# Groups of three score units instead of two, with x copied by VectorE in the first row

## Chip, cores, metric

One core of a Trainium2 chip. The time is device microseconds of one execution, the median of several. All runs used here were in the fast state, except that before_again is a single execution, whose state is not known. The calls to the chip ran on different chips, each with its own runs of before, so kernels of different calls are compared by their ratios. A ratio is the mean time of one kernel's fast runs over that of the other's fast runs of the same rounds, so it is not quite the ratio of the medians that are quoted.

## The reference

Attention with a threshold, then an MLP mixer, all in f32:

```python
# q, k, v: (8 batches, 8 heads, 576, 64)
scores = (q @ k.T) / 8
scores = where(scores >= max(scores) - tau, scores, -1e9)
attn   = softmax(scores)
x      = (attn @ v), heads side by side          # (8, 576, 512)
h      = relu(x.T @ w_tok1) @ w_tok2             # token mixer
u      = x + h.T
out    = u + relu(u @ w_ch1) @ w_ch2             # channel mixer
```

## The kernel before

Heads go in pairs. Two pairs make a quad of 2 x 576 = 1152 query rows, cut into nine **units** of 128 rows; the fifth unit is shared, 64 rows of each pair. Eight batches with two quads each are 16 quads, 144 units. I call the 18 units of one batch a **row of units**. A unit's life: TensorE makes scores, VectorE takes maxima, ScalarE makes e, GpSimd scales it. Then e must be turned, so that its keys lie on partitions. One unit later in the first row, two in the later ones, the finished group meets v in a **visit** of values, which gives x.

The first row (b=0) has no mixer work yet; there e is turned by TensorE through PSUM and copied. From the second row on it is turned in 32x32 blocks by VectorE, and 16 transfers put the blocks in place:

```python
def group_of(u):                      # units are visited two at a time, the shared one alone
    b, p0, t = units[u]
    if t == SHARED:
        return (b, p0, "s"), 0, 1
    i, c = divmod(t - (t > SHARED), NI)
    return (b, p0 + i, c // 2), c % 2, 2

def turn(u, third):                   # first row, cut
    ps = ps_tr.tile(...)              # two PSUM buffers, shared with the visits
    for c in range(3):
        nc.tensor.transpose(out=ps[:, c, :], in_=e[:, k0 : k0 + P], identity=ident)
    on = nc.scalar.copy if third == 1 and u % 2 else nc.vector.tensor_copy
    on(out=eT[...], in_=ps)

def turn_blocks(u):                   # later rows, cut
    nc.vector.transpose(out=T[...], in_=e[...])
    if place == n - 1:
        eTs[key] = work.tile([P, NK * 2 * P], F32, tag="eT")      # two buffers
        for a in range(4):
            for i in range(4):
                nc.sync.dma_start(out=eTs[key][...], in_=T[...])

def values(b, p, c):                  # a visit, cut: N = 256 columns, or 64 for the shared unit
    ps = ps_tr.tile(...)
    for h in range(2):                # the two heads: two 64-column halves of the array, side by side
        nc.tensor.matmul(to[r], lhsT=vl[:, r], rhs=eT[:, NI], start=True, ...)
    for c in range(NI):
        for h in range(2):
            nc.tensor.matmul(to[r], lhsT=lv[:, j, :], rhs=eT[:, j], ...)
    nc.scalar.copy(out=x, in_=ps)
```

One iteration of the main loop, cut to the order of work:

```python
scores(u)
values_due(u)                 # first row
norm(u - 1)
turn(w, 0..2)                 # first row, w = u - 2
fill(0.4)                     # mixer products of the batch before, from the second row on
turn_blocks(w)                # later rows
weight_to(2.25 * (u - 1.5))   # first row: a few steps of unpacking the mixer's weights, mostly VectorE
weigh(u)                      # e, with fill(0.2) between its parts
...
load_qk(...); prep(...)       # q and k of a later pair: loads, VectorE turns them
values_due(u)                 # later rows: just ahead of the next scores
```

## Time and profile before

| | before |
|---|---|
| median of the first 6 runs | 1381.45 us (1379.32 to 1383.14) |
| records of TensorE for visits | 1920 |
| transfers of e | 1120 |

The prediction shows the page's slices and where TensorE is idle. One more view is needed here: busy time in three stretches that follow the program, namely the first row of units, the second row, and the rest (from the first scores of units 0, 18 and 36). Columns: length, then busy time of TensorE, its weight loads, VectorE, ScalarE, GpSimd, then granted clock, DMA share and GB/s.

```profile
9.73:100.58 90.85, 77.67 (x504) 48.25 (x504) 71.26 (x146) 66.75 (x145) 46.20 (x84) 0.96 0.46 106
100.58:260.18 159.60, 139.28 (x731) 86.78 (x730) 113.97 (x177) 90.51 (x194) 78.70 (x105) 0.95 0.52 137
260.18:1381.30 1121.12, 1113.38 (x5636) 699.09 (x5632) 402.87 (x680) 431.71 (x989) 227.86 (x482) 1.00 0.35 85
```

In the first row VectorE is busy 71.3 of 90.9 us. What ends its idle time there, from the waits of VectorE in that window (total us, times, longest):

```profile
DVE eT L362 <- PE tr L360: 10.9, 18, 1.4
DVE mx L309 <- PE sc L304: 7.2, 6, 2.4
```

It waits for TensorE, in pieces of at most 2.4 us.

### The profile page before, as it was taken

The numbers are of one execution on the slowest core, as the hardware profiler recorded it, in microseconds if no ns is written. First come the engines' busy times: TensorE is split into PE (matmuls) and PEld (weight loads), VectorE is DVE, ScalarE is ACT, GpSimd is POOL, SyncE is SP. The second block draws the span as 40 slices with busy tenths as digits, with TensorE's granted clock in tenths as the row PEclk, the third lists the DMA queues.
The fourth block names the chain that finished last, engine by engine and source line by source line (L and its number), as shares of the span: only waits on it lengthen the run. The fifth ranks groups of instructions, "written<-read, shape, count | busy, mean of one in ns | idle before, by whom it ended". The sixth has DMA issues, their size and how long they took to land.

```text
span 1381.3 us, 19492 instructions
## 1 busy us (share of the span) xinstructions
PE 1330.3 (96%) x6866; PEld 834.1 (60%) x6866; DVE 590.3 (43%) x1009; ACT 589.5 (43%) x1328; POOL 354.8 (26%) x683
## 2 busy tenths in 40 slices
PE   6887789999999999999999999999999999999998
PEld 3544555646565666665766567565657566575675
DVE  5889875354444443434244444433343453201000
ACT  5776654445445444443434444353434454120110
POOL 3556653232323222222222222221221232100000
PEclk9988999999999999999999999999999999999999
DMA  5444654453444444433433444443333433300000
GB/s 118 109 105 120 180 150 119 109 129 89 110 121 105 98 110 101 105 81 88 109 87 93 104 95 107 99 102 81 94 90 92 110 74 88 83 8 16 8 8 23
DMA packets 257376, 128.34 MB, mean 93 GB/s; under 512 B 208064, under 2 KB 221376, under 8 KB 257280
## 3 DMA queue, kind: packets, MB, share of 16 engines
q1 hardware_dynamic: 129264, 111.16, 30.6%
q10 hardware_dynamic: 128016, 15.94, 7.3%
q8 instruction: 55, 0.90, 0.3%
q14 instruction: 41, 0.34, 0.1%
HBM read 43.25 MB, written 9.44 MB: 38 GB/s over the span
## 4 chain that ended last, share of the span: by engine, by line
PE 88%; DVE 6%; DMA 2%; SPq 1%; issue 1%; ACT 1%; POOL 1%; ACTq 0%; DVEq 0%; POOLq 0%
PE c L487 27%; PE c L471 27%; PE sc L304 11%; PE pv L416 8%; PE t L442 4%; PE t L449 4%; PE pv L411 3%; DVE mx L309 2%; PE c L483 1%; PE tx L433 1%; SPq L381 1%; PE pv_s L416 1%; DVE eT L362 1%; PE tr L360 1%; DMA eT<-T 1%
## 5 line engine op out<-in xcount | busy, mean ns | idle before, releaser
L309 DVE TENSOR_REDUCE mx<-sc 128x1 f32<-128x576 f32 x288 | 204.6, 751 | 488.6 <-PE sc L304 488.6
L471 PE MATMUL c<-xT,wc 128*128 128x256 f32 (+1 forms) x1920 | 401.0, 363 | 6.2 <-ACT g L472 5.0
L487 PE MATMUL c<-wc,g 128*128 128x512 f32 x864 | 390.7, 597 | 0.0
L471 PEld LDWEIGHTS c<-xT,wc 128*128 128x128 f32 x1920 | 335.0, 191 | 76.5 <-issue 29.0
L310 POOL TENSOR_SCALAR bias<-mx,toff 128x1 f32<-128x1 f32 x288 | 79.2, 275 | 803.1 <-DVE mx L309 746.5
L487 PEld LDWEIGHTS c<-wc,g 128*128 128x128 f32 x864 | 157.4, 190 | 175.6 <-issue 173.6
L319 ACT ACTIVATE e<-sc,bias 128x576 f32<-128x576 f32 x288 | 198.8, 739 | 141.4 <-POOL bias L310 141.2
L472 ACT ACTIVATE g<-c 128x256 f32<-128x256 f32 (+1 forms) x240 | 86.9, 362 | 328.8 <-PE c L471 315.4
L337 POOL TENSOR_SCALAR e<-e,rr 128x576 f32<-128x576 f32 x288 | 217.2, 767 | 16.8 <-DVE rr L334 4.7
L326 ACT ACTIVATE e<-e,ntau 128x576 f32<-128x576 f32 x288 | 220.8, 771 | 0.0
L304 PE MATMUL sc<-kT,qT 64*128 64x288 f32 (+1 forms) x1280 | 196.5, 441 | 15.0 <-DVE kT L286 9.7
L371 DVE STREAM_TRANSPOSE T<-e 128x1152 f32<-128x1152 f32 x126 | 172.6, 1370 | 13.3 <-DMA eT<-T 8.5
L304 PEld LDWEIGHTS sc<-kT,qT 64*128 64x128 f32 (+1 forms) x1280 | 107.3, 181 | 91.8 <-issue 44.8
L416 PE MATMUL pv<-eT,lv 128*64 128x256 f32 x1024 | 124.9, 386 | 0.0
L492 DVE COPY o<-c 128x512 f32<-128x512 f32 x36 | 24.9, 692 | 174.5 <-PE c L487 174.5
L416 PEld LDWEIGHTS pv<-eT,lv 128*64 128x64 f32 x1024 | 75.9, 140 | 39.0 <-issue 3.6
L421 ACT COPY xT<-pv 128x256 f32<-128x256 f32 x64 | 23.8, 372 | 174.8 <-PE pv L416 167.0
L449 PE MATMUL t<-w,a 128*128 128x288 f32 x256 | 75.2, 421 | 6.3 <-DVE xT L453 4.3
L442 PE MATMUL t<-x_sb,w 128*128 128x512 f32 x160 | 72.1, 597 | 0.0
L449 PEld LDWEIGHTS t<-w,a 128*128 128x128 f32 x256 | 46.0, 192 | 31.3 <-issue 11.5
L453 DVE TENSOR_TENSOR xT<-xT,t 128x288 f32<-128x288 f32 x64 | 28.2, 446 | 78.1 <-PE t L449 77.4
L326 ACT ACTIVATION_READ_ACCUMULATOR e<-e,ntau 128x1 f32 x288 | 56.6, 196 | 0.0
(48 smaller groups left out, 604.3 us busy)
## 6 DMA issues: line engine op xcount, KB each, us to landing
eT<-T SPq DMA_DIRECT2D x896, 72.0 KB, 2.0
scratch<-in_moe_w_ch_dram SPq DMA_DIRECT2D x24, 512.0 KB, 3.7
lv<-in_v_dram SPq DMA_DIRECT2D x32, 288.0 KB, 3.4
out_dram<-o SPq DMA_DIRECT2D x36, 256.0 KB, 2.1
lk<-in_k_dram ACTq DMA_DIRECT2D x112, 72.0 KB, 2.7
eT<-T SPq DMA_DIRECT2D x224, 36.0 KB, 1.9
lq<-in_q_dram ACTq DMA_DIRECT2D x104, 72.0 KB, 2.2
lq<-in_q_dram SPq DMA_DIRECT2D x24, 72.0 KB, 3.4
```

What stands on the lines that cost most here:

```text
L304: nc.tensor.matmul(sc[h][rows, f, 0:HS], lhsT=qT[r, cols], rhs=kT[r, HS * f : HS * f + HS], start=True, stop=True)
L309: nc.vector.tensor_reduce(out=mx[:, c], in_=sc[h][:, :, 0:HS], axis=AX.XY, op=ALU.max)
L319: nc.scalar.activation(out=eh, in_=sc[h][:, :, 0:HS], func=AF.Prelu, bias=bias[:, h : h + 1], scale=SCALE, alpha=STEEP)
L326: nc.scalar.activation(out=eh, in_=eh, func=AF.Exp, bias=ntau, accum_out=rs[:, h : h + 1])
L337: nc.gpsimd.tensor_scalar(out=eh, in0=eh, scalar1=rr[:, h : h + 1], scalar2=1.0, op0=ALU.mult, op1=ALU.mult)
L371: nc.vector.transpose(out=T.rearrange("p (a c n x) -> p c a n x", a=4, c=NK, n=n)[:, :, :, place, :], in_=e.rearrange("p (c a x) -> p c a ...
L416: nc.tensor.matmul(to[r], lhsT=lv[:, j, :], rhs=eT[:, j], start=False, stop=(c == NI - 1), skip_group_check=True)
L442: nc.tensor.matmul(ps, lhsT=w1[:, t, P * m : P * m + P], rhs=x_sb[:, t, :], start=(t == 0), stop=(t == NT - 1))
L449: nc.tensor.matmul(ps, lhsT=s["a"][:, m, P * c : P * c + P], rhs=w2[:, m, HS * f : HS * f + HS], start=(m == 0), stop=(m == NTK - 1))
L471: nc.tensor.matmul(ps, lhsT=wc1[:, j, c, :], rhs=uT[:, c, GR * i : GR * i + n], start=(c == 0), stop=(c == NCC - 1))
L472: nc.scalar.activation(out=s["g"][:, j, 0:n], in_=ps, func=AF.Relu)
L487: nc.tensor.matmul(flat, lhsT=s["g"][:, j, P * t : P * t + P], rhs=wc2[:, j, :], start=False, stop=(j == NJ - 1), skip_group_check=True)
```

## The change

Three units make a group, the shared one among them, so a quad has three visits instead of five: 384, 2 x 192 and 384 columns; in the shared unit the second pair now gives its first 64 rows, no longer its last. There are 48 transfers of e a quad instead of 80. Because the buffers grow, e turned has one buffer instead of two in the later rows, and q and k have one instead of two, so they are loaded later. In the first row VectorE copies x, and the weight steps stand ahead of the turning.

```diff
-    def group_of(u): ...
+    GU = 3
+    key, place = (b, p0, t // GU), t % GU
...
-    for i in range(4): ... eTs[key][32 * a : 32 * a + 32, w * i : w * i + w] <- T[32 * i : 32 * i + 32, w * a : w * a + w]
+    eT = work.tile([P, GU, 4, NK * 32], F32, tag="eT", bufs=1)
+    for i in range(4): ... eT[32 * a : 32 * a + 32, :, i, :] <- T[32 * i : 32 * i + 32, a, :, :]
...
+    SHARES = [[(0, 0, GU * P, 0)], [(0, 0, P + LAST, 2 * P + P), (1, P + LAST, P + LAST, 0)], [(1, 0, GU * P, P + LAST)]]
+    def values(b, p0, g): ... for i, first, N, tok in SHARES[g]: (ten products of N columns)
...
-        nc.scalar.copy(out=x, in_=ps)
+            if in_blocks(b):
+                nc.scalar.copy(out=x, in_=ps)
+            else:
+                copies.append(lambda x=x, ps=ps: nc.vector.tensor_copy(out=x, in_=ps))
...
         norm(u - 1)
+        weight_to(2.25 * (u - 1.5))          # first row
+        while copies: copies.popleft()()
         turn(w, 0..2)
-        weight_to(2.25 * (u - 1.5))
...
-        loaded[n] = [ld.tile([P, S // 32, 32], F32, tag=tag) ...]              # two buffers
+        loaded[n] = [ld.tile([P, S // 32, 32], F32, tag=tag, bufs=1) ...]
-        load q and k five or more units ahead, the second pair's at the very start
+        when = {3: (2, 0, 2), 4: (2, 2, 4), 5: (2, 4, 6), 6: (2, 6, 8), 8: (3, 0, 3), 0: (1, 3, 6), 1: (1, 6, 8)}
```

More of the change, by code (lines that the diff above doesn't have):

```diff
@@ L95, with load_qk @@
     vlast = [const.tile([P, P], F32, name=f"vl{i}") for i in range(VL)]
-    def load_qk(n, eng, part=None):
+    def load_qk(n, eng, parts=range(8)):
         b, p = pairs[n]
         if n not in loaded:
-            loaded[n] = [ld.tile([P, S // 32, 32], F32, tag=tag, name=f"{tag}_{n}") for tag in ("lq", "lk")]
-        for i in range(4) if part is None else (part,):
+            loaded[n] = [ld.tile([P, S // 32, 32], F32, tag=tag, bufs=1, name=f"{tag}_{n}") for tag in ("lq", "lk")]
+        for part in parts:
+            i, which = divmod(part, 2)
             h, c = divmod(i, 2)
-            for src, t, on in zip((q, k), loaded[n], eng):
-                on.dma_start(
-                    out=t[32 * i : 32 * i + 32], in_=src[b, 2 * p + h, :, 32 * c : 32 * c + 32].rearrange("(n t) d -> t n d", t=32)
-                )
+            eng[which].dma_start(
+                out=loaded[n][which][32 * i : 32 * i + 32],
+                in_=(q, k)[which][b, 2 * p + h, :, 32 * c : 32 * c + 32].rearrange("(n t) d -> t n d", t=32),
+            )
     def load_v(n):
@@ L245 @@
     load_piece(0)
-    load_qk(1, (nc.sync, nc.scalar))
-    load_piece(1)
     load_v(0)
-    for i in range(2, NRAW):
+    for i in range(1, NRAW):
         load_piece(i)
@@ L295, in scores @@
         if t == SHARED:
-            parts = [(b * NP + p0 + i, slice(MAIN, S), slice(64 * i, 64 * i + 64)) for i in range(2)]
+            parts = [(b * NP + p0, slice(MAIN, S), slice(0, 64)), (b * NP + p0 + 1, slice(0, LAST), slice(64, P))]
         else:
-            i, c = divmod(t - (t > SHARED), NI)
-            parts = [(b * NP + p0 + i, slice(P * c, P * c + P), slice(0, P))]
+            o = P * t if t < SHARED else LAST + P * (t - SHARED - 1)
+            parts = [(b * NP + p0 + (t > SHARED), slice(o, o + P), slice(0, P))]
         order = [(f, part, h) for f in range(2) for part in parts for h in range(2)]
@@ L338, in norm, with turn @@
         st[u] = e
-    def group_of(u):
+    GU = 3
+    def turn(u, third):
         b, p0, t = units[u]
-        if t == SHARED:
-            return (b, p0, "s"), 0, 1
-        i, c = divmod(t - (t > SHARED), NI)
-        return (b, p0 + i, c // 2), c % 2, 2
-    def turn(u, third):
-        key, place, n = group_of(u)
+        key, place = (b, p0, t // GU), t % GU
         e = st[u]
         if third == 0 and place == 0:
-            eTs[key] = work.tile([P, NK * 2 * P], F32, tag="eT", name=f"eT_{u}")
+            eTs[key] = work.tile([P, NK, GU * P], F32, tag="T", name=f"eT_{u}")
         if third == 2:
             st.pop(u)
-        eT = eTs[key][:, 0 : NK * n * P].rearrange("p (c x) -> p c x", c=NK)
         ps = ps_tr.tile([P, MAIN], F32, tag="tr", name=f"tr{third}_{u}")[:, 0 : 3 * P].rearrange("p (c x) -> p c x", c=3)
@@ L361, in turn @@
         on = nc.scalar.copy if third == 1 and u % 2 else nc.vector.tensor_copy
-        on(out=eT[:, 3 * third : 3 * third + 3, P * place : P * place + P], in_=ps)
+        on(out=eTs[key][:, 3 * third : 3 * third + 3, P * place : P * place + P], in_=ps)
     def turn_blocks(u):
-        key, place, n = group_of(u)
+        b, p0, t = units[u]
+        key, place = (b, p0, t // GU), t % GU
         e = st.pop(u)
         if place == 0:
-            Ts[key] = work.tile([P, NK * 2 * P], F32, tag="T", name=f"T_{u}")
-        T = Ts[key][:, 0 : NK * n * P]
+            Ts[key] = work.tile([P, 4, GU, NK * 32], F32, tag="T", name=f"T_{u}")
+        T = Ts[key]
         nc.vector.transpose(
-            out=T.rearrange("p (a c n x) -> p c a n x", a=4, c=NK, n=n)[:, :, :, place, :],
-            in_=e.rearrange("p (c a x) -> p c a x", c=NK, a=4),
+            out=T[:, :, place, :].rearrange("p a (c x) -> p c a x", c=NK), in_=e.rearrange("p (c a x) -> p c a x", c=NK, a=4)
         )
-        if place == n - 1:
+        if place == GU - 1:
             del Ts[key]
-            eTs[key] = work.tile([P, NK * 2 * P], F32, tag="eT", name=f"eT_{u}")
-            w = NK * n * 32
+            eT = work.tile([P, GU, 4, NK * 32], F32, tag="eT", bufs=1, name=f"eT_{u}")
+            eTs[key] = eT.rearrange("p n i (c x) -> p (n i) c x", c=NK)
             for a in range(4):
                 for i in range(4):
-                    nc.sync.dma_start(
-                        out=eTs[key][32 * a : 32 * a + 32, w * i : w * i + w], in_=T[32 * i : 32 * i + 32, w * a : w * a + w]
-                    )
+                    nc.sync.dma_start(out=eT[32 * a : 32 * a + 32, :, i, :], in_=T[32 * i : 32 * i + 32, a, :, :])
     def split_middle(n):
@@ L391, in split_middle, with values @@
         vals[n] = lv, vl
-    def values(b, p, c):
-        lv, vl = vals[b * NP + p]
+    copies = deque()
+    SHARES = [[(0, 0, GU * P, 0)], [(0, 0, P + LAST, 2 * P + P), (1, P + LAST, P + LAST, 0)], [(1, 0, GU * P, P + LAST)]]
+    def values(b, p0, g):
         if b not in xTs:
             xTs[b] = xTs[b + 1] = work.tile([P, NP, 2 * S], F32, tag="xT", name=f"xT_{b}")
-        key = (b, p - p % 2, c) if c == "s" else (b, p, c)
-        n, N, tok = (1, LAST, MAIN) if c == "s" else (2, 2 * P, 2 * P * c)
-        first = LAST * (p % 2) if c == "s" else 0
-        eT = eTs[key] if c == "s" else eTs.pop(key)
-        if in_blocks(b):
-            eT = eT[:, 0 : NK * n * P].rearrange("p (i c x) -> p c i x", i=4, c=NK)
-            eT = eT[:, :, first // 32 : first // 32 + N // (32 * n), :]
-        else:
-            eT = eT[:, 0 : NK * n * P].rearrange("p (c x) -> p c x", c=NK)[:, :, first : first + N]
-        ps = ps_tr.tile([P, MAIN], F32, tag="tr", name=f"pv_{b}_{p}_{c}")[:, 0:N]
-        to = ps.rearrange("p (i x) -> p i x", x=32 * n) if in_blocks(b) else ps
-        for h in range(2):
-            r = slice(D * h, D * h + D)
-            nc.tensor.matmul(to[r], lhsT=vl[:, r], rhs=eT[:, NI], start=True, stop=False, skip_group_check=True)
-        for c in range(NI):
@@ new lines, in values @@
+        eT = eTs.pop((b, p0, g))
+        whole = ps_tr.tile([P, MAIN], F32, tag="tr", name=f"pv_{b}_{p0}_{g}")
+        xs = []
+        for i, first, N, tok in SHARES[g]:
+            p = p0 + i
+            lv, vl = vals[b * NP + p]
+            ps = whole[:, first : first + N]
+            if in_blocks(b):
+                to, e = ps.rearrange("p (m x) -> p m x", x=32), eT[:, first // 32 : (first + N) // 32]
+                e = [e[:, :, j, :] for j in range(NK)]
+            else:
+                to, e = ps, [eT[:, j, first : first + N] for j in range(NK)]
@@ L413, in values @@
             for h in range(2):
                 r = slice(D * h, D * h + D)
-                j = (NI + 1) * h + c
-                nc.tensor.matmul(to[r], lhsT=lv[:, j, :], rhs=eT[:, j], start=False, stop=(c == NI - 1), skip_group_check=True)
-        x = xTs[b][:, p, S * (b % 2) + tok : S * (b % 2) + tok + N]
-        if in_blocks(b) and n == 2:
-            x = x.rearrange("p (n i x) -> p i n x", n=n, x=32)
-            ps = ps.rearrange("p (i n x) -> p i n x", n=n, x=32)
-        nc.scalar.copy(out=x, in_=ps)
+                nc.tensor.matmul(to[r], lhsT=vl[:, r], rhs=e[NI], start=True, stop=False, skip_group_check=True)
@@ new lines, in values @@
+            for c in range(NI):
+                for h in range(2):
+                    r = slice(D * h, D * h + D)
+                    j = (NI + 1) * h + c
+                    nc.tensor.matmul(to[r], lhsT=lv[:, j, :], rhs=e[j], start=False, stop=(c == NI - 1), skip_group_check=True)
+            o = S * (b % 2) + tok
+            xs.append((xTs[b][:, p, o : o + N], ps))
+        for x, ps in xs:
+            if in_blocks(b):
+                nc.scalar.copy(out=x, in_=ps)
+            else:
+                copies.append(lambda x=x, ps=ps: nc.vector.tensor_copy(out=x, in_=ps))
@@ L539, in values_due @@
         while due and due[0][0] <= u:
-            _, b, p, c = due.popleft()
-            values(b, p, c)
-            if p == NP - 1 and c == 1:
+            _, b, p0, g = due.popleft()
+            values(b, p0, g)
+            if p0 == NP - 2 and g == 2:
+                if not in_blocks(b):
+                    return True
                 push(b)
+        return False
     for u in range(len(units) + LAG + 4):
@@ L556 @@
             scores(u)
+        last = False
         if due and not in_blocks(due[0][1]):
-            values_due(u)
+            last = values_due(u)
         if 0 < u <= len(units):
@@ L563 @@
             weight(2)
+        else:
+            weight_to(2.25 * (u - 1.5))
+        while copies:
+            copies.popleft()()
+        if last:
+            push(0)
         if back:
-            key, place, many = group_of(w)
-            if not in_blocks(key[0]):
+            wb, wp, wt = units[w]
+            if not in_blocks(wb):
                 for i in range(3):
                     turn(w, i)
-            if place == many - 1:
-                b, p, c = key
-                if c == 0 and p % 2 == 0:
-                    split_middle(b * NP + p)
-                if c == "s":
-                    split_middle(b * NP + p + 1)
-                when = u + (2 if in_blocks(b) else 1)
-                due += [(when, b, p + i, c) for i in range(2 if c == "s" else 1)]
+            if wt % GU == GU - 1:
+                g = wt // GU
+                if g < 2:
+                    split_middle(wb * NP + wp + g)
+                due.append((u + (2 if in_blocks(wb) else 1), wb, wp, g))
         if b_now:
             fill(0.4)
-        if back and in_blocks(key[0]):
+        if back and in_blocks(wb):
             turn_blocks(w)
@@ L583 @@
             weight(2)
-        else:
-            weight_to(2.25 * (u - 1.5))
         if on:
@@ L597 @@
         if on:
-            m = n + 2 + t // 4
-            if t < 8 and m < len(pairs):
-                load_qk(m, (nc.scalar if b_now else nc.sync,) * 2, t % 4)
-                if t % 4 == 3:
-                    load_v(m)
+            when = {3: (2, 0, 2), 4: (2, 2, 4), 5: (2, 4, 6), 6: (2, 6, 8), 8: (3, 0, 3), 0: (1, 3, 6), 1: (1, 6, 8)}
+            if u == 0:
+                load_qk(1, (nc.sync, nc.sync), range(0, 3))
+            if t in when:
+                m, lo, hi = when[t]
+                if n + m < len(pairs):
+                    load_qk(n + m, (nc.scalar if b_now else nc.sync,) * 2, range(lo, hi))
+            if t in (3, 7) and n + 2 + t // 4 < len(pairs):
+                load_v(n + 2 + t // 4)
             if t == 2:
```

## The prediction

> **What bounds the kernel now.** I read the page first, then busy time by stretch, the waits of TensorE, the timeline of TensorE around visits of values, and the groups by shape. From the page, the engines and the 40 slices:
>
> ```profile
> PE 1330.3 (96%) x6866; PEld 834.1 (60%) x6866; DVE 590.3 (43%) x1009; ACT 589.5 (43%) x1328; POOL 354.8 (26%) x683
> ...
> PE   6887789999999999999999999999999999999998
> PEld 3544555646565666665766567565657566575675
> DVE  5889875354444443434244444433343453201000
> ACT  5776654445445444443434444353434454120110
> ...
> PEclk9988999999999999999999999999999999999999
> ```
>
> TensorE (PE) is busy nearly everywhere except in the first four or five slices, where VectorE (DVE) is the fuller engine. Busy time in four stretches of my choice (first row of units; end of weight conversion; rows 2 to 8; tail) tells it in numbers:
>
> ```profile
> 20.00:100.00 80.00, 68.04 (x478) 42.44 (x477) 66.85 (x138) 59.20 (x131) 43.42 (x77) 0.96 0.40 93
> 100.00:160.00 60.00, 44.53 (x195) 24.61 (x196) 54.52 (x88) 36.59 (x73) 38.66 (x43) 0.89 0.52 145
> 160.00:1212.00 1052.00, 1043.12 (x5528) 651.23 (x5526) 454.43 (x756) 464.42 (x1057) 267.90 (x544) 1.00 0.42 101
> ```
>
> The columns are PE, PE's weight loads, VectorE, ScalarE, GpSimd, then granted clock, DMA share and GB/s. From 160 to 1212 us PE has 1043.1 of 1052 us: 9 us idle, so there only PE's own work counts. From 20 to 100 us PE and VectorE have 85% and 84%: they take turns and neither is full. From 100 to 160 us VectorE has 91%, and is the bound. PE's whole list of waits is short, and its head lies in the first row (the transposes on PE are used there alone):
>
> ```profile
> PE tr L360 <- DVE eT L362: 14.8, 9, 5.3
> PE sc L304 <- DVE kT L286: 9.7, 1, 9.7
> PE sc L304 <- ACT e L319: 5.3, 5, 1.9
> ```
>
> No wait of PE on a transfer of e stands in that list.
>
> **What the Trainium skill says.** (1) "TensorEngine Tiling (Array Packing)", Tiling Modes, Key Properties: a change of tiling mode, not merely of tile, drains TensorE. Visits of values work in two 64-column halves while their neighbours use other shapes, so each visit should pay on entry and exit whatever its width. The trace agrees: about 0.24 us a visit, worked out below. (2) "TensorE: Matmul & The Clock Gate", Back-to-back issue gap: warm, N/2.4 + 2.5 ns for one matmul. In the trace an f32 matmul is two records, and both halves run together, so a step (one record of each half) of 256 columns should be 2 x 256/2.4 = 213 ns plus a little. Starts of single records are 215.5 ns apart; for 64 columns 58.5 ns (53.3 plus 5). It agrees. (3) Same page, The HAM clock gate: the clock halves after idle windows. The granted clock of 0.96 and 0.89 in the first two stretches against 1.00 fits.
>
> **Part 1, visits of values (PE).** The timeline of TensorE has one visit of each width:
>
> ```profile
> 571.12 3.62 PE L471 MATMUL c<-xT,wc 128*128 128x256 f32 x16
> 574.67 0.65 PE L411 MATMUL pv<-eT,vl 128*64 128x256 f32 x4
> 575.15 1.90 PE L416 MATMUL pv<-eT,lv 128*64 128x256 f32 x16
> 576.98 1.20 PE L304 MATMUL sc<-kT,qT 64*64 64x288 f32 x16
> ```
>
> ```profile
> 624.21 0.34 PE L411 MATMUL pv_s<-eT,vl 128*64 128x64 f32 x4
> 624.38 0.64 PE L416 MATMUL pv_s<-eT,lv 128*64 128x64 f32 x16
> 624.84 0.29 PE L411 MATMUL pv_s<-eT,vl 128*64 128x64 f32 x4
> 624.96 0.64 PE L416 MATMUL pv_s<-eT,lv 128*64 128x64 f32 x16
> 625.53 1.24 PE L304 MATMUL sc<-kT,qT 64*128 64x288 f32 x8
> ```
>
> From a visit's first start to the next work's start: 2.31 us wide, 1.32 us for the narrow one (two segments, one after the other). A wide visit is 10 steps of 215.5 ns = 2.16, leaving 0.15; the narrow one 20 steps of 58.5 = 1.17, again leaving 0.15. On entry the last record before it takes 309 ns instead of 216: another 0.09. So a visit costs 0.24 us, a step 0.833 ns a column plus 2 to 5 ns. Today a quad (two pairs of heads, 9 units) has four wide visits and one narrow: 4 x 2.40 + 1.41 = 11.02 us. After: two visits of 384 columns, each 10 steps of 322 = 3.22 + 0.24 = 3.46, and one of 2 x 192 columns, 20 steps of 162 = 3.24 + 0.24 = 3.49; together 10.42 us. Columns are the same (1152 x 10). **Saved: 0.60 us a quad**: two visits fewer are 0.48, and twenty narrow steps fewer about 0.1. Row b=0 has 2 of the 16 quads; the other 14 give 14 x 0.60 = 8.4 us. Of that, the first quad or so of row 2 lies in the VectorE-bound stretch and may be lost: 7.8 us of gain.
>
> **Part 2, transfers of e.** 70 groups of 16 become 42 groups of 16: 1120 issues fall to 672. They are on SyncE, 0.59 us median each, so 264 us of issuing go; nothing on PE's path waits for them. Each becomes larger (72 to 108 KB) and in pieces of 1152 bytes rather than 2304. A group takes 10.3 us from first to last issue, lands 2.05 us later, and in the trace the visit that reads it starts 2.15 to 13 us after (median 7.1). The visit is still due two units after the last transpose. With an estimated 1 us more for landing the smallest slack stays positive. The buffer becomes single, but the next group's transfers start after its third unit, half a unit or more after the visit that empties it. Cost: 0.
>
> **Part 3, single buffers for q and k, later loads.** The last load of a pair is now issued one unit before the transpose that reads it, not five. From the existing loads at the same places of the program (end of t=6 against the transpose in t=7; t=1 against t=2) the margin between landing and transpose is 1.35 to 11 us in 25 of 26 cases and -1.05 in one. VectorE has time left (454 of 1052 us), and q and k are needed a unit or two later. Cost: 0 to 1 us.
>
> **Part 4, first row.** x is copied by VectorE: per quad two copies of 384 columns (the eT copy of that size takes 0.55 us) and two of 192 (0.34, from 0.55 and the 0.69 of a 512-column copy): 1.8 us, for two quads 3.6 us more on the engine that is nearly the bound. ScalarE loses about 3.8 us. Against it, weight conversion now stands ahead of the turning of e, so VectorE has work while PE does the visit; today it waits there. Idle VectorE time from 20 to 100 us is 13 us, and five coupled visits a quad become three. PE's saving there is another 1.2 us. I take half of the idle time as recovered (6.5) less the copies (3.6): a gain of 3, with an uncertainty of 5.
>
> **Sum:** 1381.45 - 7.8 - 3 = 1370.6, less 0.5 for a little more full clock: **1370 us** (0.8% faster).
>
> **Rivals.** *First row gets slower:* if the copies simply lengthen VectorE's chain and the conversion put ahead delays the turning, +4 instead of -3: 1377. For it: VectorE is already 84 to 91% busy there. Against: the idle part is just the wait behind visits. *A wait on e takes the place of the visits:* with one eT buffer and heavier transfers, each of 42 visits could wait. At 0.5 us each that is 21 us, and 1391 in all. For it: smallest slack of 2.15 us, and 12 us of SyncE queue between transpose and landing. Against: median slack of 7.1 us, and 40% fewer issues on that queue. *Late q and k:* VectorE stalls 1 to 2 us at 28 preparations, and the maximum, ScalarE and the next scores follow: at worst +20, 1390; the margins above speak against. *First row improves much:* all 13 us of idle recovered and the slow-clock windows gone: 1360.
>
> **Range and chances.** The visit arithmetic is tight (records repeat to the nanosecond), some 8 us with an error of 1; the first row gives +4 to -10. Run to run the spread was 2.8 us. So 1361 to 1379. A gain over 2% would need 27.6 us, three times what PE sheds: 0.03. A loss over 2% needs one of the two waits at full strength: 0.02. Within 2%: 0.95.
>
> **What would show it.** Right: PE records of values fall from 1920 to 1280, visits of 3.37 and 3.39 us to the next start, the stretch from the second row to the last unit shorter by about 8 us, PE idle there still near 9 us, the tail of 170 us unchanged, the first row shorter by some 3 us with VectorE nearer to 90%. Wrong: waits of PE on transfers of e or on kT/qT in the list, VectorE waiting for q and k by more than a few us, a step of 384 columns well over 322 ns (the 128-byte pieces in which it reads e), or a first row that is longer.

## The result, and the profile after

The changed kernel takes **1380.07 us** (1376.94 to 1382.51, 6 runs) against 1381.45; ratio 0.9991, 95% interval 0.9976 to 1.0006. A repetition with more runs gave 1.0003 (0.9991 to 1.0016). So it is the same time; the 11 us of gain that I expected are missing. The profiled execution happened to be the fastest of its six (1376.94 us) and that of before one of the slower (1383.08 us), so the spans of the two profiles, 1375.1 and 1381.3 us, must not be subtracted.

From the page of the changed kernel:

```profile
PE 1322.7 (96%) x6226; PEld 817.9 (59%) x6226; DVE 588.2 (43%) x1017; ACT 581.8 (42%) x1288; POOL 356.0 (26%) x683
```

TensorE has 640 records fewer, all of visits, and 7.6 us less to do. The same three stretches, by the first scores of units 0, 18 and 36:

```profile
7.06:104.20 97.14, 78.93 (x445) 47.80 (x445) 75.09 (x158) 63.66 (x134) 53.15 (x89) 0.91 0.43 100
104.20:256.48 152.28, 134.09 (x612) 81.99 (x611) 110.46 (x172) 89.06 (x188) 74.23 (x101) 0.94 0.55 139
256.48:1375.10 1118.62, 1109.66 (x5173) 688.08 (x5172) 400.53 (x680) 427.81 (x967) 226.57 (x482) 1.00 0.37 86
```

The last two stretches are shorter, 1270.9 against 1280.7 us. The first row is longer, 97.1 against 90.9: TensorE has 1.3 us more busy time there and VectorE 3.8, and both also idle more (length less busy time: TensorE 18.2 instead of 13.2 us, VectorE 22.1 instead of 19.6). The granted clock in it fell from 0.96 to 0.91.

The visits are what was computed. The timeline of TensorE, one visit of 384 columns:

```profile
596.48 1.89 PE L470 MATMUL c<-xT,wc 128*128 128x256 f32 x8
598.30 0.87 PE L408 MATMUL pv<-eT,vl 128*64 128x384 f32 x4
599.00 2.75 PE L413 MATMUL pv<-eT,lv 128*64 128x384 f32 x16
601.67 1.24 PE L302 MATMUL sc<-kT,qT 64*128 64x288 f32 x8
```

From first start to the next work 3.37 us; a middle visit takes 3.40. Where TensorE waits now, from its list of waits:

```profile
PE tr L353 <- DVE eT L355: 17.7, 8, 3.6
...
PE pv L408 <- DMA eT<-T: 3.3, 4, 1.6
PE tr L353 <- ACT eT L355: 3.1, 5, 0.8
...
PE tr L353 <- DVE xT L420: 1.4, 5, 0.5
```

The waits on turned e being copied (tr is used in the first row, and while its last units drain) are the large ones; a wait on transfers of e is new and small. In the first row alone, before and after:

```profile
PE tr L360 <- DVE eT L362: 8.1, 7, 2.0
PE tr L353 <- DVE eT L355: 11.8, 6, 3.0
```

And VectorE's waits in the first row:

```profile
DVE mx L307 <- PE sc L302: 8.4, 8, 2.4
DVE xT L420 <- PE pv L413: 7.7, 4, 2.9
DVE eT L355 <- PE tr L353: 3.9, 11, 0.6
```

Beside before, the 10.9 us of waiting for transpositions became 3.9 us of that and 7.7 us of waiting for a visit to end. The wait was not filled; it moved. One of these visits in the timeline, VectorE and TensorE alone:

```profile
82.27 1.41 DVE L307 TENSOR_REDUCE mx<-sc 128x1 f32<-128x576 f32 x2
...
83.19 3.04 PE L413 MATMUL pv<-eT,lv 128*64 128x384 f32 x16
...
83.87 0.41 DVE L201 TENSOR_SCALAR wc<-scratch 128x512 uint32<-128x512 uint32 x1
...
86.26 0.56 DVE L420 COPY xT<-pv 128x384 f32<-128x384 f32 x1 [1.99 <-PE pv L413]
```

VectorE finishes the weight step at 84.3 and then idles 1.99 us until the visit ends, because its next instruction in order is the copy of x.

### The profile page after: what moved, and what is told of

Same layout as the page of the kernel before. It is cut to its first block, busy times and chain, and to the rows that moved or that the text cites. A ratio compares the mean times of both kernels' runs of the same rounds, so it can differ in the third digit from the quotient of the medians.

```text
span 1375.1 us, 17691 instructions
## 1 busy us (share of the span) xinstructions
PE 1322.7 (96%) x6226; PEld 817.9 (59%) x6226; DVE 588.2 (43%) x1017; ACT 581.8 (42%) x1288; POOL 356.0 (26%) x683
## 4 chain that ended last, share of the span: by engine, by line
PE 85%; DVE 7%; DMA 2%; SPq 2%; ACT 1%; issue 1%; POOL 1%; ACTq 0%; DVEq 0%; POOLq 0%
PE c L486 26%; PE c L470 26%; PE sc L302 11%; PE pv L413 9%; PE t L441 5%; PE t L448 3%; PE pv L408 3%; DVE mx L307 2%; SPq L374 2%; PE tx L432 1%; PE c L482 1%; DMA eT<-T 1%; PE tr L353 1%; DVE wc L205 1%; ACT e L317 1%
## 5 line engine op out<-in xcount | busy, mean ns | idle before, releaser
L308 POOL TENSOR_SCALAR bias<-mx,toff 128x1 f32<-128x1 f32 x288 | 82.8, 288 | 799.3 <-DVE mx L307 742.3
L302 PE MATMUL sc<-kT,qT 64*128 64x288 f32 (+1 forms) x1280 | 196.6, 447 | 11.1 <-DVE kT L284 7.1
L413 PE MATMUL pv<-eT,lv 128*64 128x384 f32 (+1 forms) x1024 | 136.8, 409 | 0.0
L418 ACT COPY xT<-pv 128x384 f32<-128x384 f32 (+1 forms) x56 | 21.0, 401 | 157.5 <-PE pv L413 157.5
```

The source lines that it names most:

```text
L302: nc.tensor.matmul(sc[h][rows, f, 0:HS], lhsT=qT[r, cols], rhs=kT[r, HS * f : HS * f + HS], start=True, stop=True)
L413: nc.tensor.matmul(to[r], lhsT=lv[:, j, :], rhs=e[j], start=False, stop=(c == NI - 1), skip_group_check=True)
```

## The experiments

All kernels gave correct results. To compare traces I use the time between the first scores of units 0, 18 and 36 and the end, read from TensorE's records. The first scores started 7.0 to 9.8 us after the start in all kernels, whatever their loads; that difference is left out. A stretch does not hold the same visits in every kernel: before has 200, 240 and 1480 records of visits in the three, the changed kernel 140, 120 and 1020. With the durations of visits above, an estimate is 0.4 us more visiting in the changed first row, 4.2 us less in the second and 2.7 us less in the rest.

| trace | first row | second row | rest | of first row at half clock |
|---|---|---|---|---|
| before, before_again | 90.9, 92.2 | 159.6, 157.5 | 1121.1, 1121.1 | 6.8, 10.2 |
| changed, after_again | 97.1, 99.6 | 152.3, 153.2 | 1118.6, 1118.7 | 17.1, 27.3 |
| late_only, late_only_2 | 90.4, 93.6 | 154.2, 153.6 | 1116.4, 1116.4 | 3.4, 17.1 |
| order_only, order_only_2 | 91.2, 88.7 | 153.9, 153.5 | 1116.4, 1116.4 | 6.8, 0.0 |
| x_vector, x_vector_2 | 93.3, 91.7 | 154.9, 153.8 | 1116.4, 1116.4 | 6.8, 3.4 |
| x_scalar | 96.4 | 152.3 | 1118.3 | 10.2 |
| old_loads | 95.9 | 154.6 | 1117.3 | 10.2 |
| old_order | 95.5 | 152.8 | 1119.0 | 10.2 |
| threes | 97.3 | 153.6 | 1118.4 | 10.2 |
| halves | 90.9 | 162.1 | 1124.0 | 6.8 |
| halves_push | 89.2 | 152.8 | 1116.7 | 3.4 |
| ones | 88.6 | 154.9 | 1117.7 | 3.4 |
| apart | 91.1 | 157.0 | 1128.6 | 6.8 |

**after_again** (no edit).

> The changed kernel, unedited, for a second trace and a tighter time. The first profiled run of it (1375.1 us span) was the fastest of six, the others 3 us longer. Theory A (the first two rows of units lose what the visits save): 1380 us, ratio to before 0.999; from the scores of unit 36 to the end the trace agrees with the first trace of the changed kernel (about 1118.6 us) within 1.5 us, and any difference in length lies ahead of unit 36. Theory B (the waits on transfers of e and on q and k in the later rows eat the saving, by chance less in the first trace): the stretch after unit 36 is 2 us or more longer than in the first trace, with more waits of TensorE on transfers of e than 3.3 us.

1381.43 us, 14 runs, ratio 1.0003. The stretch after unit 36 repeats within 0.1 us, and all but 0.1 of the 3.7 us between the two spans lies ahead of unit 36. So the later rows are steady and the early ones are where executions differ: theory A.

**late_only**: the kernel before, with groups of three from the second row on alone.

```diff
 def group_of(u):
     b, p0, t = units[u]
+    if b > 0:
+        return (b, p0, t // GU), t % GU, GU
...                                       # first row: turn(), values() and copies as before
-            values(b, p, c)
+            (values3 if b else values)(b, p, c)
-    small = tc.tile_pool(name="small", bufs=6)
+    small = tc.tile_pool(name="small", bufs=5)    # else 32 bytes a partition are missing
```

> Before, with groups of three units from the second row of units on alone (loads, first row and ScalarE's copies as before; one small pool has 5 buffers instead of 6 so that it fits). Theory A: all of the visits' saving as the first trace shows it, 0.40 us a quad and 14 quads, 5.6 us: 1376 us, ratio 0.996. Theory B: with the same single buffer for e and the same transfers as the changed kernel it gains no more than that one, 1380 us, ratio 0.999.

1370.8 us, ratio **0.9933** (0.992 to 0.9946): 9 us gained of the 11 that I had predicted, by leaving the first row alone. Theory B falls: the single buffer for e and the fewer, larger transfers are in this version too. The gain is larger than the 5.6 us that theory A gave it.

**x_scalar**: the changed kernel, x of the first row copied by ScalarE.

```diff
-                copies.append(lambda x=x, ps=ps: nc.vector.tensor_copy(out=x, in_=ps))
+                nc.scalar.copy(out=x, in_=ps)
```

> The changed kernel, but x of the first row is copied by ScalarE right after each visit, as before. Theory A1 (VectorE's copy in the chain between a visit and the turning of e costs the first row; 8 to 12 copies of 0.34 to 0.55 us and the wait of VectorE for the visit, 7.7 us in the trace): the first row is 3 us or more shorter, 1377 us. Theory A2 (the lumps of longer visits and the half-clock windows they bring cost it, whoever copies): within 1 us of the changed kernel, 1380 us.

1376.29 us, ratio 0.9970 (0.9961 to 0.998), against 1.0003 of the changed kernel in the same call: 4.5 us. In the traces the first row is 0.7 and 3.2 us shorter. Time and expectation of A1 agree, though 5 us still lack to late_only.

**old_loads**: the changed kernel with two buffers for q and k and the loads of before.

```diff
-            loaded[n] = [... bufs=1 ...]
+            loaded[n] = [... ]                     # two, and small with 5 buffers
-    load_piece(0); load_v(0)
+    load_piece(0); load_qk(1, (nc.sync, nc.scalar)); load_piece(1); load_v(0)
-            when = {3: (2, 0, 2), ...}
+            m = n + 2 + t // 4                     # one part a unit, t = 0..7
```

> The changed kernel with the loads of q and k as before: two buffers each, the second pair's loads up front, the others five units ahead (small pool with 5 buffers to fit). Theory C (single-buffered q and k stall VectorE and through it TensorE): 2 us or more faster than the changed kernel, 1378 us or less. Theory A: no gain after the start, and the first scores again 2.7 us later (9.7 instead of 7.1 us after the start), so 1380 to 1383 us.

1380.97 us, ratio 0.999 (0.9975 to 1.0005). Theory C falls: the later, single-buffered loads cost nothing that the time shows. Its rest is 1.3 us shorter than that of the changed kernel, with no wait of TensorE for e in it, so about 1 us may be theirs. My guess about the start was wrong too, the first scores came at 7.0 us.

**before_again** (no edit, one look).

> The kernel before, unedited, for a second trace. The four variants that ran so far all issue their first scores 7.05 to 7.5 us after the start, one of them with the start of the kernel before, whose first trace has 9.7. Theory A: that was a matter of that one execution, so the second trace of before starts them at about 7.1 us, and from unit 36 to the end it repeats 1121.1 us within 1 us. Rival: the start belongs to the kernel, 9.7 us again.

First scores at 9.5 us, so theory A's guess that the first trace was an accident did not hold for this pair; but late_only, with the same loads at its start, had 7.1 and halves_push 9.8, so the start varies and does not follow the change. What sets it is open. The rest repeats 1121.1.

**order_only**: late_only, with the weight steps ahead of the turning.

```diff
             norm(u - 1)
         if b_now:
             weight(2)
+        else:
+            weight_to(2.25 * (u - 1.5))
...
-        else:
-            weight_to(2.25 * (u - 1.5))
         if on:
             weigh(u)
```

> The version with groups of three from the second row on alone (1370.8 us), plus one thing of the changed kernel's first row: the weight conversion stands ahead of the turning of e. Theory D (this order costs the first row, since TensorE's third transposition of a unit waits for VectorE's first copy of turned e, which now stands behind a conversion step of 0.3 to 1.3 us): first row 4 us or more longer than its 90.4 us, TensorE's waits on the copies of turned e up from 10.2 us to 14 or more, time 1374 to 1376 us. Rival E (the wider visits in groups of three are what costs): within 1 us of 1370.8.

1369.62 us, ratio 0.9911 (0.9897 to 0.9925); first row 91.2. Theory D falls clearly: TensorE's waits on VectorE's copies of turned e did rise, from 8.1 us in late_only's first row to 11.1, but the row is not longer.

**x_vector**: late_only, with x copied by VectorE in the first row.

```diff
-        nc.scalar.copy(out=x, in_=ps)
+        copies.append(lambda: nc.vector.tensor_copy(out=x, in_=ps))      # run after norm, ahead of turn
```

> The version with groups of three from the second row on alone (1370.8 us), plus VectorE copying x in the first row, with the old order and the groups of two. Twelve copies, four wide ones of about 0.4 us and one pair of 0.2 us a quad. Theory A1 (the copy on VectorE costs some 4 us, as between the changed kernel and the one with ScalarE's copies): 1374 to 1376 us. Rival: it costs only together with the other order, where a conversion step delays it, then 1371 to 1372 us here.

1374.05 us, ratio 0.9937 (0.9922 to 0.9951). Above order_only of the same call (0.9911), but level with late_only of the earlier one (0.9933): not settled by this call.

**old_order**: x_scalar, with the weight steps after the turning again.

```diff
-            weight_to(2.25 * (u - 1.5))            # ahead of turn
+            weight_to(2.25 * (u - 1.5))            # after turn_blocks, as before
```

> The changed kernel with x on ScalarE and with the weight conversion after the turning of e again; of its first row only the groups of three and the later loads remain. Theory D (order): the first row falls from 96 to about 91 us, time 1371 us. Rival E (the groups of three in the first row): the first row stays near 96 us, time 1375 to 1377 us.

1376.74 us, ratio 0.9956 (0.9938 to 0.9973); first row 95.5. With order and x's copy undone, the first row is still 3 to 5 us too long. With the loads excluded by old_loads, that leaves the groups of three: rival E.

**threes**: old_loads with x on ScalarE. Of the changed first row, the groups of three and the order remain; order_only differs from it in the groups and in what goes with them (which rows the shared unit takes, and that the mixer's work is queued a little later in the program).

```diff
-                copies.append(lambda x=x, ps=ps: nc.vector.tensor_copy(out=x, in_=ps))
+                nc.scalar.copy(out=x, in_=ps)
```

> The changed kernel with the loads of before and x on ScalarE: against the fastest version so far (order_only, 1369.6 us, first row 91.2 us) the groups of three in the first row are the only thing of the changed first row added. Theory E (the wider visits, 3.4 us in one lump every three units instead of 2.3 and 1.3 us spread over five of nine, cost the first row although their work is less): first row 94 us or more, 1373 to 1375 us. Rival (the late loads were it, with their wait of 1.5 us on q): first row at most 92 us, 1370 us.

1377.1 us, ratio 0.9967 (0.9953 to 0.9982); first row 97.3. Its first row in the stretches, and VectorE's waits there:

```profile
8.71:106.01 97.30, 78.56 (x445) 48.48 (x445) 73.09 (x151) 66.49 (x143) 52.87 (x89) 0.95 0.45 103
```

```profile
DVE eT L357 <- PE tr L355: 13.7, 14, 4.2
DVE mx L309 <- PE sc L304: 8.5, 7, 2.4
```

VectorE has about the work of before (73.1 us) and 24.2 us of idle time, with single waits of up to 4.2 us behind a visit.

**halves**: threes, with each visit of the first row in two halves of 192 columns, one unit apart.

```diff
-                due.append((u + (2 if in_blocks(wb) else 1), wb, wp, g))
+                if in_blocks(wb):
+                    due.append((u + 2, wb, wp, g, None))
+                else:
+                    due += [(u + 1, wb, wp, g, 0), (u + 2, wb, wp, g, 1)]
```

> As threes, but each visit of the first row is done in two halves of 192 columns in two consecutive units; groups of e stay groups of three. Two visits' fixed cost more per group, about 0.2 us each and six a quad. Theory E (lumps): the first row falls back to 90 to 92.5 us although TensorE has more to do, 1370 to 1372 us. Rival E2 (something else about groups of three, such as x or e coming later): stays with threes, 94 us or more.

The first row fell to 90.9 us as theory E has it, but the time rose to 1387.47 us, ratio 1.0037 (1.0022 to 1.0052). The last visit came a unit later, and so did the start of the mixer's work: unit 21 alone took 17.6 us, the second row 162.1, and the rest 1124.0. As a test by time it failed, by my own edit.

**halves_push**: the same with the last visit whole.

```diff
                 if in_blocks(wb):
                     due.append((u + 2, wb, wp, g, None))
+                elif wp == NP - 2 and g == 2:
+                    due.append((u + 1, wb, wp, g, None))
```

> As halves, but the very last visit of the first row is whole, so that the mixer's work of that row starts in unit 20 as in every other version (in halves it started in unit 21, and the row after took 162 us instead of 154). Theory E (lumps cost the first row): first row about 91 us as in halves, the row after 152 to 155 us, and the time 1370 to 1373 us, 4 us or more below threes (1377.1). Rival (the halves gain nothing, the first row of halves was luck or is paid back in the row after): 1376 us or more.

1370.88 us, ratio **0.9922** (0.9907 to 0.9937), 6 us below threes, with more visits and more records for TensorE.

```profile
9.83:99.03 89.20, 73.61 (x484) 48.56 (x485) 73.20 (x151) 67.31 (x145) 52.23 (x87) 0.98 0.48 111
```

```profile
DVE mx L309 <- PE sc L304: 7.8, 6, 2.4
DVE eT L357 <- PE tr L355: 7.0, 17, 0.9
```

VectorE's busy time is that of threes to 0.1 us, and its waits behind transpositions are 7.0 us instead of 13.7, none over 0.9. The granted clock is 0.98. Of the 8.1 us by which the first row is shorter, some 1.7 are one half visit that now falls after unit 18; the 6.4 that remain agree with the time. This shows that the undivided visits (the lumps) cost the first row, not the groups. The second half also comes a unit later, and no run moves an undivided visit later, so dividing and delaying are not told apart.

**ones**: order_only with groups of one unit in the first row.

```diff
-        return (b, p0 + i, c // 2), c % 2, 2
+        return (b, p0 + i, c), 0, 1
-        n, N, tok = ... (2, 2 * P, 2 * P * c)
+        n, N, tok = ... (1, P, P * c)
```

> As order_only, with groups of one unit in the first row, ten visits a quad of 128 (and two times 64) columns. TensorE's work rises by about 4 visits x 0.24 us a quad, and ScalarE's copies of x from six to ten. Theory E (lumps) carried on: the first row becomes 88 to 91 us, 1367 to 1370 us. Rival (work counts, not lumps): 93 us, 1372 us.

First row 88.6 us, the shortest of all, in line with theory E. The time, 1372.78 us and ratio 0.9928 (0.9913 to 0.9942), is no better than order_only's; the rest took 1117.7 instead of 1116.4 us. So the time missed its expectation, and the gain of the row was given back later: 1.2 us of the rest is one wait of a visit, which the list puts down to a transfer of the output; otherwise where is not settled.

**apart**: order_only, with the later rows' visits between mixer products.

```diff
             fill(0.4)
+        if due and in_blocks(due[0][1]):
+            values_due(u - 1)
...
-        if due and in_blocks(due[0][1]):
-            values_due(u)
```

> As order_only, but the visits of the later rows stand between products of the mixer instead of just ahead of the next scores. The trace of before shows that a product followed by scores takes 309 ns, as one followed by a visit does, so ahead of scores a visit pays no entry of its own. Theory F (a visit that stands alone pays entry and exit, 0.09 us more each; that is why a removed visit gave 0.40 us a quad and not 0.60): 42 x 0.09 = 3.9 us longer, 1373.5 us; the time of TensorE's records shows it at each visit. Rival: no difference, 1369.6 us; or the visit, which empties the only buffer of e later, makes TensorE wait on transfers of e.

1385.58 us, ratio 1.0028 (1.0014 to 1.0042): 16 us slower than order_only by the medians. The sign is theory F's, the size is four times it. After unit 36 TensorE changes its tiling 299 times instead of 267; 32 x 0.093 = 3.0 us of the 12.2 us by which that stretch grew. TensorE's idle time grew by 3.8 us there (from 3.3 to 7.1); the other 5.3 us are busy time that is not accounted for, and 3.8 us of the stretch ran at half clock, none in order_only. Inconclusive as a measure of the entry; what it does show is that the place of a visit, with the later time that goes with it, is worth more than its fixed cost.

**late_only_2, x_vector_2, order_only_2** (no edits): the three side by side on one chip.

> The version with groups of three from the second row on alone, again, beside x_vector and order_only on one chip: ratio to before 0.992 to 0.993, first row 90 to 91.5 us.

> The same with x of the first row copied by VectorE. Theory A1 (the copy on VectorE costs on its own): first row 2 to 3 us longer than late_only's, ratio 0.0015 or more above it. Rival (it costs only beside the wide visits of groups of three, where VectorE waits for the visit): ratio within 0.001 of late_only's.

> The same as late_only with the weight conversion ahead of the turning. If the order matters by itself its ratio differs from late_only's by 0.0015 or more; the two earlier ratios (0.9911 and 0.9933) came from different chips, and their first rows differ by 0.8 us only, so I expect no difference that the interval shows.

1370.26, 1373.63 and 1369.64 us; ratios 0.9926, 0.9947 and 0.9922, intervals of +-0.002. Order: no difference. VectorE's copies: 0.0021, or 3 us, over the threshold of A1 but with overlapping intervals; the earlier call had x_vector 0.0026 above order_only, so I take about 3 us as likely and not as shown. The expected first row of late_only failed: 93.6 us instead of 90 to 91.5, with 17.1 us at half clock instead of 3.4.

The fastest versions are order_only (1369.6 us), late_only and halves_push; between them nothing is decided. Each beats both kernels by some 10 us.

## Why the prediction was wrong

**Part 1, visits: the size of the later rows' gain held, its composition partly.** The new visits took 3.37 and 3.40 us to the next start, 3.37 and 3.39 predicted. What failed is the entry of 0.09 us charged to every visit. In the trace of before a 256-column product followed by a visit starts 309 ns ahead of it, and one followed directly by scores also 309 ns, against 216 to another product. The visit stands ahead of scores, which need their own change of tiling, so that 0.09 us stays when the visit goes. TensorE's time in visits fell from 10.55 to 10.15 us a quad: 0.40, not 0.60, hence 5.6 us for 14 quads and not 8.4. Still, the later rows gave the 7.8 us predicted, or more: with the first row left as it was, late_only gained 0.67%, 9 us. That the size agrees is luck, since the visits give 5.6 of it. From the visits that each stretch holds, an estimate is that late_only's second row should lose 3.0 us and its rest 2.7; they lost 4.6 and 4.7 (means of two traces). One wait that went is to be seen in before: 1.3 us of scores on ScalarE, ahead of 312 us. The others are not accounted for one by one.

**Part 2, transfers: nearly right.** 672 issues, 0.60 us each, landing after 2.2 us instead of 2.0. The smallest slack between landing and visit fell from 2.15 to 0.09 us, and TensorE waited 3.3 us for e in all, where I had put 0: 1.6 us in the second row and 1.7 after unit 36. The rest took 1118.6 instead of late_only's 1116.4 us, and 1.9 of these 2.2 us are idle time of TensorE. late_only and order_only have the same transfers and wait for e too, 1.9 and 2.0 us, but in the second row alone, so it looks like a matter of timing and not of the transfers' cost.

**Part 3, q and k: right.** I had put 0 to 1 us; old_loads gained nothing that the time shows, and 1.3 us in the rest of its trace.

**Part 4, first row: the step that failed.** Its second term failed: VectorE's idle time recovered, at -6.5 us. The first term, the copies at +3.6, was right: VectorE's busy time in the first row rose by 3.8 us, 3.1 of it seven copies of x (the eighth falls after unit 18). The second had the wrong sign: its idle time rose, from 19.6 to 22.1 us (in the second trace of each kernel from 21.1 to 24.3), and the row from 91.5 to 98.4 us (means of two traces each), +6.8. I had reasoned that weight steps ahead of the turning would fill the wait behind a visit. They do, for 0.4 us in the visit shown; but the visit had grown from 2.3 to 3.4 us, and VectorE, taking its instructions in the program's order, then stands before a copy of x which needs the visit's end. With x on ScalarE it stands before the copy of a transposition that TensorE does after the visit (threes: 13.7 us, up to 4.2 at a time). TensorE's own waits on copies of turned e, 14.8 us in before, I had read as the first row's; 8.1 of them are, the rest are two waits after unit 18. In the first row they rose to 11.8. What the runs put in place of the recovery:

- The lumps. All six traces with undivided visits of three units have first rows of 95.5 to 99.6 us; the twelve traces with groups of two, groups of one, or halves have 88.6 to 93.6. Over the first two rows together, where the boundary at unit 18 does not matter, the six have 248.3 to 252.8 us, and the others with groups of three in the later rows 242.0 to 248.2, halves left out. halves_push against threes: 8.1 us of first row, 6 us of time, at equal work for VectorE.
- The copies of x on VectorE: 4.5 us together with the lumps (x_scalar against after_again), and likely some 3 us without them. The times say so; the traces do not place it: old_loads, with these copies, has a first row of 95.9 us, and threes, without them, one of 97.3.
- Not the order of the weight steps, and not the loads of q and k.

Half-clock windows add to it: the first row spent 17.1 and 27.3 us in them in the changed kernel, 6.8 and 10.2 before. late_only's two traces differ by 13.7 us of half clock and by 3.2 us of first row, which by an estimate from these two gives 0.23 us a microsecond, so 3 of the 6.8 us; the other pairs of traces of one kernel give 0.24 to 0.47, so up to 6. But at equal half clock the rows still differ: with 10.2 us of it before_again has 92.2 us and the four traces with undivided visits of three 95.5 to 97.3; with 17.1 us late_only_2 has 93.6 and the changed kernel 97.1. So some 3 to 5 us are not the clock. What brings the windows about stays open.

The rival "first row gets slower" was right in its sign, with +4 where +7 came, and in the copies; the order, its other reason, cost nothing, and the undivided visit was not in it. I gave it too little weight because I took an idle engine's time as available without asking in what order its instructions come.

**Sum:** the later rows about -8 and the first row about +7 leave -1, where I had -7.8 and -3.

## What to carry to other kernels

Before merging small work into larger pieces, look at each stage for what bounds it. In this kernel, where TensorE was full, fewer and wider pieces paid their fixed cost back; where two engines took turns with little buffering between them, a longer piece was a longer wait for the other, and the split version with more visits was faster. VectorE's idle time could only be filled by what stood ahead of the wait in its own order. And the fixed cost read ahead of a visit belonged to the change of mode, so check what follows when the operation is gone.

## What the Trainium skill lacked or had wrong

- "TensorEngine Tiling (Array Packing)", Tiling Modes, Key Properties: says that a change of mode drains TensorE, but not what it costs. Here a product ahead of a change takes 309 instead of 216 ns (256 columns) or 523 instead of 429 ns (512 columns), 0.093 us each time, whether a visit or scores follow. A product ahead of a transposition of 64 columns, which the trace lists as `128*64` like a visit, takes 216 ns, so a narrower tile alone costs nothing here. And taking an operation from between two others of different modes saves one change, not two.
- "TensorE: Matmul & The Clock Gate", Back-to-back issue gap: gives the gap of one pass, and no page gives a time for an f32 product. For f32 in two 64-column halves a step is 2N/2.4 plus 2 to 5 ns: 58.5, 162.5, 215.5 and 322.3 ns for 64, 192, 256 and 384 columns, and the first step of a visit some 50 ns more.
- Same page, The HAM clock gate: ties half rate to an idle window of about 3.4 us. In the first row of before the longest wait of TensorE after its first scores is 2.0 us, and yet 6.8 us of it ran at half clock. A later section of the page, on a second failure mode, says that frequent short idle times bring half rate too; what it lacks is how many. Part 4 of the page says that transpositions do not count as busy in the same way. The first row has 144 records of them, but the stretch after unit 36 has 276 among other products, at a granted clock of 1.00; no run here separates this.
